# Score products of low queries: over the high keys alone, as pairs of 64-row tiles of the array

## The chip, the cores and the metric

The kernel runs on one core of a Trainium2 chip. The metric is the device time of one execution in microseconds, here the median of several runs.

## What is computed

The reference is an attention over pooled queries, followed by two MLPs in a row. Cut to what matters:

```python
def _attn_ref(q, k, v):                 # q, k, v: (2, 8, 1152, 64)
    q_pool = q.reshape(B, H, S // 2, 2, D).mean(axis=3)
    scores = np.matmul(q_pool, k.transpose(0, 1, 3, 2)) / np.sqrt(D)
    scores = scores - np.max(scores, axis=-1, keepdims=True)
    attn = np.exp(scores)
    attn = attn / (np.sum(attn, axis=-1, keepdims=True) + 1e-09)
    return np.matmul(attn, v)           # (2, 8, 576, 64)
...
x = attn_out.transpose(0, 2, 1, 3).reshape(1152, 512)
x = _moe_ref(x, w_in, w_out)            # ELU between two products, 512 -> 2048 -> 512
return _moe2_ref(x, moe2_w_in, moe2_w_out)   # the same with h * tanh(log(1 + e^h))
```

## The kernel before

The kernel wants more than one rounding to float32r gives. So each operand of a product is split into a high part, the value rounded to float32r, and a low part, what is left of it, and products of the parts are added up in PSUM.

The attention takes the 16 heads in eight pairs (`n`), and each pair in 9 steps (`s` = 9n + t) of 128 queries: steps t = 0 to 3 are queries of the first head, 5 to 8 of the second, and step 4 has 64 of either, for which a block of zeros in the other half is multiplied too. A step has these parts, each a function of class `Attention`:

- `scores` (L298 to L315): the products of the step's 128 queries with all 1152 keys of the head. The keys fall into three chunks, each with its own bank of PSUM: 448 and 450 columns into the two banks of the tile `wide` (two such tiles take turns), and the last 256 into half a bank, `rest` (the halves take turns by steps). The second chunk repeats two keys of the next one.
- `maxima` (L322, L325, on VectorE, DVE): the maximum over `rest` is put beside the other scores, then the maximum over all.
- `exps` (L337 over `rest`, L339 over `wide`, on ScalarE, ACT).
- `turn` and `split_a`: nine transposes per step on TensorE (PE), L370, from the tile `a` to `pst`; their results are split into `th` and `tl` by ACT with DVE or GpSimd (POOL).
- `values` (L410): products with v, 72 per pair, scattered over the steps.

For the scores the head dimension of 64 fills half of the array's 128 rows. The other half is used for the parts of the keys. `KS[h]` holds, for head h, the high parts of the keys in 64 partitions and the low parts in the other 64 (for h = 0 the high ones are partitions 0 to 63, for h = 1 they are 64 to 127); `QH` and `QL` hold the high and the low part of the queries, each stacked twice. So a product of `QH` with `KS` over 128 rows is high queries by high and low keys in one, and that of `QL` with `KS` is low queries by both. A chunk is two products:

```python
            for o, (w, x) in enumerate(ops):
                nc.tensor.matmul(dst, w, x[:, cols], start=(o == 0), stop=(o == len(ops) - 1))
```

`ops` holds `QH` and then `QL` (in step 4 these two for either head), so that a step is six products (twelve in step 4) in the order high, low for each chunk.

`KS` is filled by `stack_k` (L278) with DMAs on SyncE's queue (SP) from tiles `kh` and `kl`, a head at a time, during the pair before: as soon as the last step that reads the old keys is behind. The first pair's keys are written straight by ACT and DVE.

What stands where on each engine is set by a table, `PP['x']`: every piece of work has a due time in steps, and `run` sorts all pieces by it and emits them in that order. The engines PE, ACT, DVE, POOL and SP then run them in order, and wait for one another by semaphores. In the table `W` is the due time of the first two chunks of a step's scores (-1.236 steps) and `R` that of the third (-1.201); nothing of another kind falls between the two in the steps shown. Beside the attention run loads of MLP weights and their conversion from float64 bits (`Weights`), some of them stored to DRAM for later.

The MLPs that follow are bound together by lines L714 (products up) and L734 (down).

Of the kernel before, what the change touches and what calls it, by code (L numbers as in the profile page):

```python
# [10 lines left out]
F32 = mybir.dt.float32  # L11
F32R = mybir.dt.float32r
# [5 lines left out]
PSUM = bass.MemoryType.PSUM  # L18
# [49 lines left out]
    'ncs': 17,  # L68
    'nw': 2,
    'na_': 2,  # L70
    # where each piece of work stands in the order of emission: in steps of 128 queries, for a step, a pair of heads or a weight tile
# [38 lines left out]


class Attention:
    """Two heads at a time; queries j*64+p stand for pooled row 9p+j, keys j*128+p for token 9p+j."""

    def __init__(self, nc, tc, ctx, q, k, v, ident, xh, xl, ps2, ps1):
        self.nc, self.q, self.k, self.v = nc, q, k, v
        self.ident, self.xh, self.xl = ident, xh, xl
        self.ps2, self.ps1 = ps2, ps1
        pool = lambda name, bufs: ctx.enter_context(tc.tile_pool(name=name, bufs=bufs))
        self.raw = pool("raw", 1)  # L120
        self.tmp = pool("tmp", 2)
        self.ap = pool("aprob", PP["na_"])
        self.tiny = pool("tiny", 4)
        self.aTp = pool("aT", 2)
        self.dram = ctx.enter_context(tc.tile_pool(name="dram", bufs=2, space=bass.MemoryType.DRAM))
        fix = pool("fix", 1)
        self.QH = [fix.tile([P, 2, 704], F32R, name=f"qh{i}") for i in range(2)]
        self.QL = [fix.tile([P, 2, 704], F32R, name=f"ql{i}") for i in range(2)]
        self.KS = [fix.tile([P, S], F32R, name=f"ks{h}") for h in range(2)]
        self.VS = [fix.tile([P, 2, NKT, 2, D], F32R, name=f"vs{i}") for i in range(2)]  # L130
        for i in range(2):
            for t in (self.QH[i], self.QL[i]):
                nc.gpsimd.memset(t[:, 0, SQ:].bitcast(F32), 0.0)
        self.pairs = [(b, c) for b in range(B) for c in range(NPAIR)]
        self.rawqk = {}
        self.turned = {}
        self.rawv = {}
        self.qp = {}
        self.kT = {}
        self.wide = {}  # L140
        self.rest = ps1.tile([P, 512], F32, tag="rest", name="rest", bufs=1)
        self.neg = {}
        self.sums = {}
        self.prob = {}
        self.aT = {}
        self.xf = {}
        self.av = {}
        self.avlo = {}
        self.R = {}
        self.rec = {}  # L150
        self.nav = {}
# [12 lines left out]
        self.rawqk[n] = (qr, kr)  # L164

    def warm(self, n):
        """Products that nobody reads, so that TensorE's clock is up when the first heads arrive."""
        nc = self.nc
        z = self.tmp.tile([P, 3, P], F32, name="whole", bufs=PP["nw"])
        nc.vector.memset(z[:], 0.0)  # L170
        zb = z.rearrange("p a b -> p (a b)").bitcast(BF16)
        ps = self.ps2.tile([P, 2, 512], F32, tag="wide", name="wide")
        for i in range(n):
            nc.tensor.matmul(ps[:, 0], zb[:, :P], zb[:, :512], start=True, stop=True)
# [11 lines left out]
        self.nc.vector.tensor_tensor(self.qp[n][heads], qr[:, :, 0, :], qr[:, :, 1, :], op=ALU.add)  # L186

    def split(self, hi, lo, x):
        """hi = x rounded to float32r, lo = what is left, on GpSimd."""
        nc = self.nc  # L190
        nc.gpsimd.tensor_scalar(hi, x, 1.0, 1.0, op0=ALU.mult, op1=ALU.mult)  # L191
        nc.gpsimd.tensor_tensor(lo, x, hi.bitcast(F32), op=ALU.subtract)  # L192
# [42 lines left out]
            nc.vector.tensor_tensor(kl, ps[:, :CH], kh.bitcast(F32), op=ALU.subtract)  # L235

    def first_q(self, h, c, part):
        """The queries of the first pair, a head at a time."""
        nc = self.nc
        key = 0, "q", h, c  # L240
        if part == 0:
            self.turned[key] = ps = self.ps1.tile([P, 512], F32, tag="ps1", name="psq")
            w = 64 + 64 * h
            for i in range(3):
                nc.tensor.transpose(ps[0:64, i * w:(i + 1) * w], self.qp[0][:w, 3 * c + i, :], self.ident[:w, :w])
            return
        src = self.turned[key][0:64, :192 + 192 * h].rearrange("p (j h x) -> p h j x", j=3, x=64)[:, h]
        scale = 0.5 / math.sqrt(D)
        for r in (0,) if h else (0, 64):
            hi, lo = (x[0][r:r + 64, h, 192 * c:192 * c + 192].rearrange("p (j x) -> p j x", x=64) for x in (self.QH, self.QL))  # L250
            if part == 1:
                nc.scalar.activation(hi, src, AF.Copy, scale=scale)
            else:
                nc.vector.scalar_tensor_tensor(out=lo, in0=src, scalar=scale, in1=hi.bitcast(F32),
                                               op0=ALU.mult, op1=ALU.subtract)

    def first_k(self, h, c, part):
        """The keys of the first pair, straight from PSUM."""
        nc = self.nc
        key = 0, "k", h, c  # L260
        m, r = slice(64 * h, 64 * h + 64), slice(64 - 64 * h, 128 - 64 * h)
# [9 lines left out]
            nc.vector.tensor_tensor(self.KS[h][r, cols], self.turned[key][m, :CH], self.KS[h][m, cols].bitcast(F32), op=ALU.subtract)  # L271

    def stack_k(self, n, h):
        """The high and low parts of a head's keys, one above the other."""
        kh, kl = self.kT[n]
        m, r = slice(64 * h, 64 * h + 64), slice(64 - 64 * h, 128 - 64 * h)
        for rows, src in ((m, kh), (r, kl)):
            self.nc.sync.dma_start(self.KS[h][rows, :].bitcast(F32), src[m, :].bitcast(F32))  # L278

    def split_v(self, n, c, part):  # L280
        nc = self.nc
# [10 lines left out]
                (nc.gpsimd if 'vlo' in PP['pl'] else nc.vector).tensor_tensor(lo, vr[:, h, js, :], hi.bitcast(F32), op=ALU.subtract)  # L292

    def part(self, s):
        """Where the scores of the last keys go."""
        return self.rest[:, RW * (s % 2):RW * (s % 2) + RW]

    def scores(self, s, chunks):  # L298
        nc = self.nc
        n, t = divmod(s, 9)  # L300
        QH, QL, KS = self.QH[n % 2], self.QL[n % 2], self.KS
        if t < 4:
            ops = [(Q[:, 0, t * P:(t + 1) * P], KS[0]) for Q in (QH, QL)]
        elif t == 4:
            ops = [(Q[:, 0, 512:640], KS[0]) for Q in (QH, QL)]
            ops += [(Q.rearrange("p h x -> p (h x)")[:, 640:768], KS[1]) for Q in (QH, QL)]
        else:
            ops = [(Q[:, 1, 64 + (t - 5) * P:64 + (t - 4) * P], KS[1]) for Q in (QH, QL)]
        if 0 in chunks:
            self.wide[s] = self.ps2.tile([P, 2, 512], F32, tag="wide", name="wide")  # L310
        for i in chunks:
            cols = (slice(0, WW), slice(WW, 2 * WW + 2), slice(2 * WW, S))[i]
            dst = self.wide[s][:, i, :cols.stop - cols.start] if i < 2 else self.part(s)
            for o, (w, x) in enumerate(ops):
                nc.tensor.matmul(dst, w, x[:, cols], start=(o == 0), stop=(o == len(ops) - 1))  # L315

    def maxima(self, s, part):
        """The maximum of the last keys joins the others' scores, where the second bank repeats a key."""
        nc = self.nc
        wide, rest = self.wide[s], self.part(s)  # L320
        if part == 0:
# [18 lines left out]
                                 bias=neg[:], accum_out=self.sums[n][:, t, 0:1])  # L340

    def reciprocals(self, n, part):
        """1 / (sum + 1e-9), a row of them per head, over the partitions that the head's x has."""
        nc = self.nc
        if part == 0:
            sums = self.sums[n]
# [50 lines left out]
                nc.vector.tensor_tensor(l, src[:, :, x0:x0 + w], h.bitcast(F32), op=ALU.subtract)  # L397

    def values(self, n, g, j0, j1):
        """Some of the keys of one of the four products with v."""  # L400
        nc = self.nc
        h, c0, w = GROUPS[g]
        hi, lo = self.aT[n, g]
# [35 lines left out]
    def run(self, aside):  # L439
# [6 lines left out]
        ev = []  # L446
        add = lambda k, b, f, *a: ev.append((b + X[k], f, a))
        for s in range(T):
            add('W', s, self.scores, s, (0, 1))
            add('R', s, self.scores, s, (2,))  # L450
            add('m', s, self.maxima, s, 0)
            add('M', s, self.maxima, s, 1)
            add('e', s, self.exps, s, 0)
# [47 lines left out]


class Lag:
    """Chains of instructions that follow the products, a link of each chain per step."""

    def __init__(self):
        self.chains = []
# [8 lines left out]


class Weights:
    """Tiles of the float64 weights (MLP m, 0 = in or 1 = out, 128 of the hidden units): to float32, that to two float32r parts."""

    def __init__(self, nc, src, raw, wt, dram, lag):
        self.nc, self.src, self.rawp, self.wt, self.dram, self.lag = nc, src, raw, wt, dram, lag
# [16 lines left out]
        self.loaded[key] = t  # L539

    def chain(self, key, store=False):
        """float64 bits to float32 (clamped to its range), and that to DRAM or to its parts."""
        nc = self.nc
        if key not in self.loaded:
            self.load(key)
# [50 lines left out]
def build(ctx, tc, q, k, v, w1_in, w1_out, w2_in, w2_out, out):  # L596
# [70 lines left out]
        return [link(a, b) for a, b in zip(e, e[1:])]  # L667

    def elu(i, h, gh, gl):
        """max(e^min(h, 0) - 1, h), as e^h - 1 >= h."""  # L670
        e = tmp.tile([P, ZM], F32, name="e")[:, :h.shape[1]]
        return cut([
            lambda: nc.scalar.activation(e[:], h, AF.Relu, scale=-1.0),
# [3 lines left out]
            lambda: nc.vector.tensor_tensor(gl, h, gh.bitcast(F32), op=ALU.subtract)], PP['ec'])  # L677

    def mish(i, h, gh, gl):
        """h * n / (n + 2) with n = e^h (e^h + 2), which is h * tanh(log(1 + e^h))."""  # L680
        e, n, p = (tmp.tile([P, ZM if x == "e" else max(PP['z2'])], F32, name=x)[:, :h.shape[1]] for x in "enp")
        stt = nc.vector.scalar_tensor_tensor
        return cut([
# [138 lines left out]
```

## Time and profile before

| | us |
|---|---|
| median of 3 runs | 702.21 |
| lowest and highest | 702.15, 703.5 |
| span of the profiled execution | 701.6 |
| PE busy in the span | 676.2 |
| DVE busy | 610.0 |
| ACT busy | 484.2 |
| POOL busy | 262.2 |

The profile is of one execution. Its span goes from the first to the last instruction. The attention stage lies between about 12 and 290 us of it, the MLPs behind that. Matmuls overlap one another: a product's recorded time is longer than the distance to the next one's start, and a busy PE may still have room, so that distances between starts are to be read where a cost is wanted. PEld is the load of a product's stationary operand, which runs ahead of the product.

### The profile page before, as it was taken

The numbers are of one execution on the slowest core, as the hardware profiler recorded it, in microseconds if no ns is written. First come the engines' busy times: TensorE is split into PE (matmuls) and PEld (weight loads), VectorE is DVE, ScalarE is ACT, GpSimd is POOL, SyncE is SP. The second block draws the span as 40 slices with busy tenths as digits, with TensorE's granted clock in tenths as the row PEclk, the third lists the DMA queues.
The fourth block names the chain that finished last, engine by engine and source line by source line (L and its number), as shares of the span: only waits on it lengthen the run. The fifth ranks groups of instructions, "written<-read, shape, count | busy, mean of one in ns | idle before, by whom it ended". The sixth has DMA issues, their size and how long they took to land.

```text
span 701.6 us, 12014 instructions
## 1 busy us (share of the span) xinstructions
PE 676.2 (96%) x4043; PEld 613.3 (87%) x4043; DVE 610.0 (87%) x1142; ACT 484.2 (69%) x1180; POOL 262.2 (37%) x328
## 2 busy tenths in 40 slices
PE   7999999999999998799999999999989999999996
PEld 4898989888988897688888999999978999999995
DVE  5899999999999997789798977886999988888884
ACT  5999999999999998575555444666555554445443
POOL 2678787777778787153210000134030000000000
PEclk8999999999999999999999999999999999999999
DMA  8747485867486440456546667565220010002001
GB/s 178 201 119 194 123 199 140 193 172 186 113 198 176 114 141 31 141 191 188 189 149 193 186 185 221 176 195 166 60 75 16 1 45 1 1 0 46 1 1 45
DMA packets 62508, 86.89 MB, mean 124 GB/s; under 512 B 22696, under 2 KB 39152, under 8 KB 62448
## 3 DMA queue, kind: packets, MB, share of 16 engines
q1 hardware_dynamic: 62448, 86.14, 45.3%
q8 instruction: 32, 0.52, 0.3%
q14 instruction: 28, 0.23, 0.1%
HBM read 60.56 MB, written 12.88 MB: 105 GB/s over the span
## 4 chain that ended last, share of the span: by engine, by line
PE 68%; ACT 15%; DVE 10%; issue 3%; DMA 2%; POOL 1%; SPq 0%; ACTq 0%; POOLq 0%
PE acc L734 26%; PE up L714 25%; PE pst L370 5%; PE psv L410 5%; ACT a L339 4%; PE wide L315 3%; ACT whole L385 2%; ACT th L395 2%; ACT a L337 1%; DVE neg L325 1%; ACT wt L555 1%; PE rest L315 1%; DVE tl L397 1%; DVE wt L560 1%; DVE wt L558 1%
## 5 line engine op out<-in xcount | busy, mean ns | idle before, releaser
L714 PE MATMUL up<-xh,wh 128*128 128x384 f32 (+2 forms) x384 | 130.0, 338 | 3.7 <-ACT wh L575 2.7
L714 PE MATMUL up<-xh,wl 128*128 128x384 f32 (+2 forms) x384 | 129.6, 338 | 0.0
L714 PE MATMUL up<-xl,wh 128*128 128x384 f32 (+2 forms) x384 | 129.4, 337 | 0.0
L577 POOL TENSOR_TENSOR wl<-wt,wh 128x512 fp32r<-128x512 f32 x38 | 50.9, 1352 | 208.6 <-ACT wh L575 97.1
L192 POOL TENSOR_TENSOR tl<-whole,th 128x384 fp32r<-128x384 f32 (+1 forms) x112 | 112.2, 1001 | 9.3
L370 PE MATMUL pst<-ident,a 128*128 128x128 f32 x648 | 101.6, 276 | 7.8 <-DVE tl L397 2.6
L370 PEld LDWEIGHTS pst<-ident,a 128*128 128x128 f32 x648 | 75.1, 140 | 19.1 <-ACT a L339 7.7
L410 PE MATMUL psv<-th,vs 128*128 128x256 f32 (+1 forms) x288 | 85.9, 319 | 0.7 <-DVE xf L425 0.5
L714 PEld LDWEIGHTS up<-xh,wh 128*128 128x128 f32 x384 | 72.8, 189 | 8.9 <-ACT wh L575 3.1
L191 POOL TENSOR_SCALAR th<-whole 128x384 fp32r<-128x384 f32 (+1 forms) x112 | 60.6, 541 | 50.7 <-ACT whole L385 50.6
L410 PE MATMUL psv<-tl,vs 128*128 128x256 f32 (+1 forms) x288 | 79.1, 296 | 0.0
L325 DVE TENSOR_REDUCE neg<-wide 128x1 f32<-128x898 f32 x72 | 77.8, 1080 | 0.2
L714 PEld LDWEIGHTS up<-xl,wh 128*128 128x128 f32 x384 | 72.8, 189 | 4.6
L714 PEld LDWEIGHTS up<-xh,wl 128*128 128x128 f32 x384 | 72.6, 189 | 2.9 <-DVE wl L577 0.2
L339 ACT ACTIVATE a<-wide,neg 128x896 f32<-128x896 f32 x72 | 73.3, 1018 | 2.4 <-DVE neg L325 2.0
L687 ACT ACTIVATE e<-n 128x384 f32<-128x384 f32 x48 | 25.2, 526 | 64.9 <-DVE n L686 64.9
L555 ACT ACTIVATE wt<-raw 128x512 f32<-128x512 f32 x64 | 43.3, 679 | 37.8 <-DMA raw<-in_moe_w_out_dram 25.9
L397 DVE TENSOR_TENSOR tl<-pst,th 128x384 fp32r<-128x384 f32 (+1 forms) x128 | 59.9, 497 | 7.6 <-ACT th L395 5.6
L315 PE MATMUL wide<-ks,qh 128*128 128x448 f32 (+1 forms) x160 | 64.9, 406 | 0.0
L734 PE MATMUL acc<-gl,wh 128*128 128x512 f32 (+2 forms) x192 | 64.5, 336 | 0.0
L734 PE MATMUL acc<-gh,wl 128*128 128x512 f32 (+2 forms) x192 | 64.5, 336 | 0.0
L734 PE MATMUL acc<-gh,wh 128*128 128x512 f32 (+2 forms) x192 | 64.4, 335 | 0.0
(89 smaller groups left out, 1695.6 us busy)
## 6 DMA issues: line engine op xcount, KB each, us to landing
raw<-in_moe_w_in_dram SPq DMA_DIRECT2D x32, 512.0 KB, 4.4
raw<-in_moe_w_out_dram SPq DMA_DIRECT2D x32, 512.0 KB, 4.3
w<-wt SPq DMA_DIRECT2D x40, 256.0 KB, 4.1
wt<-w SPq DMA_DIRECT2D x40, 256.0 KB, 2.8
qr<-in_q_dram SPq DMA_DIRECT2D x16, 288.0 KB, 3.9
kr<-in_k_dram SPq DMA_DIRECT2D x16, 288.0 KB, 5.0
vr<-in_v_dram SPq DMA_DIRECT2D x8, 576.0 KB, 3.9
ks<-kh SPq DMA_DIRECT2D x14, 288.0 KB, 3.3
```

What stands on the lines that cost most here:

```text
L191: nc.gpsimd.tensor_scalar(hi, x, 1.0, 1.0, op0=ALU.mult, op1=ALU.mult)
L192: nc.gpsimd.tensor_tensor(lo, x, hi.bitcast(F32), op=ALU.subtract)
L315: nc.tensor.matmul(dst, w, x[:, cols], start=(o == 0), stop=(o == len(ops) - 1))
L325: nc.vector.tensor_reduce(neg[:], wide[:, :, :WW + 1], axis=AX.XY, op=ALU.max, negate=True)
L339: nc.scalar.activation(a[:, :2 * WW].rearrange("p (c x) -> p c x", c=2), wide[:, :, :WW], AF.Exp, bias=neg[:], accum_out=self.sums[n][:, t ...
L370: nc.tensor.transpose(ps[:, i * P:(i + 1) * P], a[:, j * P:(j + 1) * P], self.ident[:])
L397: nc.vector.tensor_tensor(l, src[:, :, x0:x0 + w], h.bitcast(F32), op=ALU.subtract)
L410: nc.tensor.matmul(ps[:, :w], self.VS[n % 2][:, h, j].rearrange("p a d -> p (a d)"), t[:, j, :w], start=(c == 1), stop=(c == 2 * NKT))
L555: lambda: nc.scalar.activation(t[:], high.bitcast(F32), AF.Abs),
L577: e.tensor_tensor(l[:], t[:], h[:].bitcast(F32), op=ALU.subtract)
L714: nc.tensor.matmul(ps[:, :z], w, x, start=(o == 0), stop=(o == len(ops) - 1))
L734: nc.tensor.matmul(ps[:, :x.shape[1]], a, x, start=(i == 0 and o == 0), stop=(i == NFF - 1 and o == 2))
```

## The change

The low queries multiply the high keys only; the product of low queries and low keys is left out, except in the first pair and in step 4 of each pair, where the old products stay. A product of high keys and low queries needs 64 of the array's rows. The first and the third chunk take the rows on which the head's high keys stand in `KS`; for the second chunk a copy of the high keys (450 columns) stands in a new tile `KX` on the other 64 partitions, and `stack_k` fills it with one more DMA for each head of a pair. The products that are 64 rows high carry a tile size of 64 by 128 and a tile position of row 0 or row 64. In all steps the three chunks' products with `QH` now come first and those with `QL` behind them, all at the due time `W`; the entry `R` is gone. The diff without lines that only lose a comment:

```diff
     'x': {
-        'W': -1.236328125, 'R': -1.2011709213256836, 'm': -0.5839824676513672, 'M': 0.07031536102294922, 'e': 0.7480506896972656,
+        'W': -1.236328125, 'm': -0.5839824676513672, 'M': 0.07031536102294922, 'e': 0.7480506896972656,
...
+        self.KX = fix.tile([P, WW + 2], F32R, name="kx")
...
         for rows, src in ((m, kh), (r, kl)):
             self.nc.sync.dma_start(self.KS[h][rows, :].bitcast(F32), src[m, :].bitcast(F32))
+        self.nc.sync.dma_start(self.KX[r, :].bitcast(F32), kh[m, WW:2 * WW + 2].bitcast(F32))
...
-    def scores(self, s, chunks):
+    def scores(self, s):
...
         if t < 4:
-            ops = [(Q[:, 0, t * P:(t + 1) * P], KS[0]) for Q in (QH, QL)]
+            ops = [(0, lambda Q: Q[:, 0, t * P:(t + 1) * P])]
         elif t == 4:
-            ops = [(Q[:, 0, 512:640], KS[0]) for Q in (QH, QL)]
-            ops += [(Q.rearrange("p h x -> p (h x)")[:, 640:768], KS[1]) for Q in (QH, QL)]
-        else:
-            ops = [(Q[:, 1, 64 + (t - 5) * P:64 + (t - 4) * P], KS[1]) for Q in (QH, QL)]
-        if 0 in chunks:
-            self.wide[s] = self.ps2.tile([P, 2, 512], F32, tag="wide", name="wide")
-        for i in chunks:
-            cols = (slice(0, WW), slice(WW, 2 * WW + 2), slice(2 * WW, S))[i]
-            dst = self.wide[s][:, i, :cols.stop - cols.start] if i < 2 else self.part(s)
-            for o, (w, x) in enumerate(ops):
-                nc.tensor.matmul(dst, w, x[:, cols], start=(o == 0), stop=(o == len(ops) - 1))
+            ops = [(0, lambda Q: Q[:, 0, 512:640]), (1, lambda Q: Q.rearrange("p h x -> p (h x)")[:, 640:768])]
+        else:
+            ops = [(1, lambda Q: Q[:, 1, 64 + (t - 5) * P:64 + (t - 4) * P])]
+        self.wide[s] = self.ps2.tile([P, 2, 512], F32, tag="wide", name="wide")
+        cols = (slice(0, WW), slice(WW, 2 * WW + 2), slice(2 * WW, S))
+        dst = [self.wide[s][:, 0, :WW], self.wide[s][:, 1, :WW + 2], self.part(s)]
+        todo = []
+        for h, q in ops:
+            for i in range(3):
+                todo.append((i, q(QH), KS[h][:, cols[i]]))
+        for h, q in ops:
+            m, r = slice(64 * h, 64 * h + 64), slice(64 - 64 * h, 128 - 64 * h)
+            for i in range(3):
+                if n == 0 or t == 4:
+                    todo.append((i, q(QL), KS[h][:, cols[i]]))
+                elif i == 1:
+                    todo.append((i, q(QL)[r], self.KX[r, :]))
+                else:
+                    todo.append((i, q(QL)[m], KS[h][m, cols[i]]))
+        left = [sum(x[0] == i for x in todo) for i in range(3)]
+        full = list(left)
+        for i, w, x in todo:
+            nc.tensor.matmul(dst[i], w, x, start=(left[i] == full[i]), stop=(left[i] == 1))
+            left[i] -= 1
...
-            add('W', s, self.scores, s, (0, 1))
-            add('R', s, self.scores, s, (2,))
+            add('W', s, self.scores, s)
```

On PE, in a step of the second head of the third pair (the products of the step follow the last transposes of a pair's queries, L199), before (`ks_114` is `KS[1]`, `qh_109` and `ql_111` are `QH` and `QL` of the even pairs):

```order
L370 MATMUL pst<-ident,a 128x128 x6
L199 MATMUL psq<-ident,qp 64x128 x6
L370 MATMUL pst<-ident,a 128x128 x3
L315 MATMUL wide<-ks_114,qh_109 128x448
L315 MATMUL wide<-ks_114,ql_111 128x448
L315 MATMUL wide<-ks_114,qh_109 128x450
L315 MATMUL wide<-ks_114,ql_111 128x450
L315 MATMUL rest<-ks_114,qh_109 128x256
L315 MATMUL rest<-ks_114,ql_111 128x256
```

And the same place of the changed kernel:

```order
L386 MATMUL pst<-ident,a 128x128 x6
L200 MATMUL psq<-ident,qp 64x128 x6
L386 MATMUL pst<-ident,a 128x128 x3
L330 MATMUL wide<-ks_114,qh_109 128x448
L330 MATMUL wide<-ks_114,qh_109 128x450
L330 MATMUL rest<-ks_114,qh_109 128x256
L330 MATMUL wide<-ks_114,ql_111 128x448
L330 MATMUL wide<-kx,ql_111 128x450
L330 MATMUL rest<-ks_114,ql_111 128x256
```

The three high products moved ahead of the three low ones, and the low product of 450 columns reads `kx`; what stands around the six is the same.

On SP's queue, where the keys of the second pair are stacked for its second head, before (`raw` and `w` belong to the MLP weights, `vr` is v, `qh` and `ql` are the queries' second copy):

```order
L535 DMA raw_611<-in_moe_w_in_dram 128x4x256
L216 DMA qh1_110<-qh1_110 64x2x576
L216 DMA ql1_112<-ql1_112 64x2x576
L582 DMA w0_0_4_641<-wt_459 128x512
L278 DMA ks1_114<-kh_305 64x1152
L278 DMA ks1_114<-kl_306 64x1152
L179 DMA vr_763<-in_v_dram 128x2x576
```

And in the changed kernel:

```order
L280 DMA kx_115<-kh_306 64x450
L550 DMA raw_613<-in_moe_w_in_dram 128x4x256
L217 DMA qh1_110<-qh1_110 64x2x576
L217 DMA ql1_112<-ql1_112 64x2x576
L597 DMA w0_0_4_643<-wt_460 128x512
L279 DMA ks1_114<-kh_306 64x1152
L279 DMA ks1_114<-kl_307 64x1152
L280 DMA kx_115<-kh_306 64x450
L180 DMA vr_766<-in_v_dram 128x2x576
```

One copy to `kx` stands behind the two copies to `ks` of each head, and ahead of a load of weights or of v; the rest of the queue has its old order. PE's first reader of `kx` in each head, steps 0 and 5, waits for that copy. DVE, ACT and POOL have the same instructions in the same order as before.

## Rows read from the trace of the kernel before

**Rows 1.** The page: span, and the chain that ended last by engine.

```profile
span 701.6 us, 12014 instructions
...
PE 68%; ACT 15%; DVE 10%; issue 3%; DMA 2%; POOL 1%; SPq 0%; ACTq 0%; POOLq 0%
```

**Rows 2.** Stages: us from:to, length, busy us of each engine, clock, DMA share, GB/s.

```profile
300.00:700.00 400.00, 393.54 (x2124) 359.24 (x2122) 336.45 (x637) 215.73 (x455) 50.92 (x38) 1.00 0.34 101
```

**Rows 3.** One period in stretches; busy us: PE, PEld, DVE, ACT, POOL.

```profile
79.50:83.10 3.60, 3.60 (x28) 3.53 (x27) 3.09 (x9) 3.34 (x10) 3.23 (x5) 1.00 0.27 41
83.10:86.50 3.40, 3.40 (x28) 3.32 (x27) 3.34 (x7) 3.20 (x9) 1.89 (x3) 1.00 0.39 152
86.50:90.00 3.50, 3.50 (x30) 3.44 (x29) 3.50 (x6) 3.31 (x10) 3.33 (x5) 1.00 0.61 171
...
98.50:102.30 3.80, 3.44 (x24) 2.54 (x22) 3.52 (x9) 3.76 (x14) 1.93 (x4) 1.00 0.99 222
102.30:105.80 3.50, 3.50 (x25) 3.42 (x26) 3.31 (x9) 3.23 (x11) 2.64 (x6) 1.00 0.43 99
105.80:109.00 3.20, 3.20 (x25) 3.13 (x24) 3.20 (x6) 2.97 (x9) 1.81 (x3) 1.00 0.43 93
```

**Rows 4.** The chain in order of time: start us, us, engine, tile, line, count.

```profile
46.97 0.81 PE wide L315 x4
...
80.07 0.81 PE wide L315 x4
...
87.59 1.00 ACT a L339 x2
...
102.80 0.82 PE wide L315 x4
...
274.75 0.82 PE wide L315 x4
```

**Rows 5.** Timeline of PE: start us, us, then what, [idle before].

```profile
102.25 0.55 PE L370 MATMUL pst<-ident,a 128*128 128x128 f32 x3
...
103.04 0.37 PE L315 MATMUL wide<-ks,qh 128*128 128x450 f32 x1
103.25 0.37 PE L315 MATMUL wide<-ks,ql 128*128 128x450 f32 x1
103.45 0.28 PE L315 MATMUL rest<-ks,qh 128*128 128x256 f32 x1
103.57 0.28 PE L315 MATMUL rest<-ks,ql 128*128 128x256 f32 x1
103.69 0.32 PE L410 MATMUL psv<-th,vs 128*128 128x320 f32 x1
...
104.57 0.49 PE L370 MATMUL pst<-ident,a 128*128 128x128 f32 x3
...
106.96 0.28 PE L315 MATMUL rest<-ks,qh 128*128 128x256 f32 x1
...
109.28 0.45 PE L315 MATMUL wide<-ks,qh 128*128 128x448 f32 x1
```

**Rows 6.** Timeline of PEld, the loads, where the columns of the array change.

```profile
116.42 0.09 PEld L353 LDWEIGHTS psr<-ident,rec 128*9 128x9 f32 x1
116.52 0.19 PEld L315 LDWEIGHTS wide<-ks,qh 128*128 128x128 f32 x1
...
127.14 0.25 PEld L199 LDWEIGHTS psq<-ident,qp 128*64 128x64 f32 x3 [0.56 <-ACT whole L385]
127.39 0.36 PEld L370 LDWEIGHTS pst<-ident,a 128*128 128x128 f32 x3
```

**Rows 7.** Timeline of ACT, the exponentials over `rest`.

```profile
105.55 0.48 ACT L337 ACTIVATE a<-rest,neg 128x256 f32<-128x256 f32 x1
```

**Rows 8.** SP's timeline at a copy of the keys, and L278's time to landing.

```profile
96.54 0.54 SPq L278 DMA_DIRECT2D ks<-kl  x1
...
DMA to landing us min/median/max: 3.1/5.0/7.9
```

## The prediction, made before the changed kernel ran

> **What bounds the kernel now.** I read the page's first lines and its chain first [rows 1]. TensorE (PE) holds 68% of the chain that ended last, ScalarE (ACT) 15%, VectorE (DVE) 10%. The change touches only the score products of the attention stage, 12 to 275 us of the span; the MLPs behind it, where PE is busy 393.54 of 400 us [rows 2], see none of it and only move with the stage's end. So the question is what bounds the attention stage. That stage repeats itself every 33.1 us, a pair of heads in 9 steps. I took one such period in stretches of a step or two and compared the busy time of the engines in each [rows 3]: in 79.5 to 86.5 us and in 102.3 to 109 us PE is busy all the time, in 86.5 to 90 us PE (3.50 of 3.50) and DVE (3.50) both are, in 98.5 to 102.3 us PE idles 0.36 us while ACT is busy 3.76 of 3.80. The chain of waits says the same [rows 4]: in the period it runs through the score products at 80.07 and 102.80 us (and again one step after each), and through ACT's exponentials at 87.59 us in between. The bound alternates: PE for about 15 of 33 us, ACT for most of the rest, with DVE hardly behind.
>
> The reader is to see two things there. PE's time is worth something, but only in the steps whose score products lie on the chain. From 46.97 us, the first in a pair that the change touches, to 274.75 us the chain has 23 pieces "PE wide L315 x4"; the first and the last stand in [rows 4]. The changed products are in 56 steps (7 pairs with 8 steps each; the first pair and the fifth step of each pair keep the old form).
>
> **What is removed: 450 columns per step, if the pair runs side by side.** The six products of a step start 0.20 us apart with 448 or 450 columns (103.04, 103.25, 103.45) and 0.12 us apart with 256 (103.45, 103.57, 103.69) [rows 5]. The three low ones so cost 0.20 + 0.20 + 0.12 = 0.52 us. After the change the 448- and the 256-column products use one half of the array's rows, the 450-column one the other half. If the halves work at the same time, the first half needs 0.20 + 0.12 = 0.32 us. The second half needs its own weights: loads of 128 columns can follow each other 0.10 to 0.11 us apart (116.42 to 116.52 [rows 6]), so it ends at 0.11 + 0.20 = 0.31 us, inside the first half's time. That saves 0.20 us of PE per step. No trace here shows two products side by side, so this is the bound on the good side; on the other there is no saving, since in-order products of 64 rows have as many columns as before. I take the good side for the likeliest, because the two write different banks and read different partitions, so nothing in the program orders them.
>
> **What is added: two changes of the array's shape per step.** From 128 rows to 64 ahead of the low products, and back behind them. The nearest rows are changes of the number of columns: the load of the transposes at 127.39 us follows the three 64-column loads at 127.14 us, and the 128-column load at 116.52 us follows that of 9 columns at 116.42 us [rows 6]. The three loads of 64 columns take 0.25 us to the next shape's load, 0.10 us from the 9-column one to the next: the pace of loads within one shape, and no idle time is printed on either row. By these a change of shape costs nothing, and I take 0. Changes of the number of rows happen before only in the first pair's start, always behind a wait, and tell nothing. The other bound is that PE must run empty at each change. A 256-column product is recorded for 0.28 us while the next one starts after 0.12 us [rows 5]: a tail of 0.16 us that would be laid open. Then the first load is uncovered as after a wait: three transposes take 0.55 us behind one (102.25) and 0.49 us without (104.57) [rows 5], 0.06 us. That is 0.22 us per change, 0.44 us per step.
>
> The Trainium skill (TensorEngine Tiling, Array Packing; Key Properties) says that changing the tiling mode, not just the tile, drains the TensorE. The column changes above don't agree with it as a general rule; for rows no trace here shows it. By the rule the sum would be that of rival 1.
>
> **What is moved.** The low products come behind all high ones, so the last-keys product with the high queries is third instead of fifth, 0.4 us earlier. It waits for ACT to have read the same half of that bank two steps before. In one step ACT's activation starts at 105.55 us and takes 0.48 us, and the product starts at 106.96 us [rows 5, 7]: 0.93 us spare, 0.5 left. No cost. The last product of the step stays the same, so DVE's maxima, which need all three banks, start no earlier within the step. DVE's, ACT's and GpSimd's own instructions keep their order.
>
> **KX.** Each pair brings two more DMAs of 115 KB on SP's queue, behind the copies of the keys (L278). One such issue takes 0.54 us of the queue and a copy of 288 KB lands in 3.1 to 7.9 us [rows 8]. The first head's last copy is issued at 96.54 us, so KX would be at about 97.1 us and there by 105.0 us even at 7.9; its first reader is in the step that starts at 109.28 us [rows 5]. 14 copies of 0.115 MB are 1.6 MB of 86.9, so I put the traffic at nothing. The second head's reader is five steps away. If that cover were gone, its price is SP's 0.54 us twice per pair, 7.6 us in all at the very most.
>
> **The sum.** 23 steps on the chain by 0.20 us are 4.6 us, the most that this chain can give. What is late next is DVE or ACT. In 79.5 to 86.5 us two steps save 0.40 us, ACT has 0.46 us of idle time there and DVE 0.57 [rows 3]: all of it can be had. In 102.3 to 109 us they save 0.40 us, ACT has 0.50 us, but DVE only 0.19: half. So 0.59 of 0.80 us is left, 4.6 x 0.59 / 0.80 = 3.4 us. An engine that leads still idles a little (ACT is busy 3.31 of 3.50 us in 86.5 to 90 us, where the chain is on it [rows 3, 4]), so not all of this room can be filled; I take three quarters, a choice: 2.6 us. The span before is 701.6 us [rows 1] and the median 702.2, 0.6 us apart; taking the saving off the median gives 699.6 us. The case spans 697.6 us (all 4.6) to 701.5 us.
>
> **Rivals.**
> 1. Row changes drain the array: +0.44 - 0.20 = +0.24 us of PE per step. The 23 steps on the chain pay 5.5 us. Of the other 33, two in a pair (14) are covered by PE's idle time, as in 98.5 to 102.3 us; 19 have none (86.5 to 90 us: 3.50 of 3.50) and pay 0 to 4.6 us. So 5.5 to 10 us, about 7: 709 us. It decides from 0.10 us per change on, where two changes eat the 0.20 us. [...] Against it: the column changes cost nothing.
> 2. The pair doesn't run side by side, and the changes are cheap: the change doesn't do what it says, PE does the same 1154 columns, only in another order: 702.2 us. The same comes out if a change costs about 0.1 us or if DVE takes over everywhere: within 1.4 us.
> 3. KX or the earlier last-keys product becomes a wait: up to 7.6 us by the bound above, more likely 2: 704 us. The margins of 4 us and 0.5 us speak against it.
>
> The Trainium skill (TensorE: Matmul & The Clock Gate, Part 3) reports that products in different row groups start about 4 ns apart and that four of 32 rows ran 3.07 times as fast. No run here shows it; by it the pair would again take 0.32 us with the third product.
>
> **How the numbers follow.** The forecast has 0.45, drains 0.30, no saving 0.20, KX or the moved product 0.05. The kernel's runs can tell about 0.2%, 1.4 us. Faster by more: 0.40 of the forecast's 0.45, and 0.03 of the others. Within it: 0.05 of the forecast, 0.17 of the others. Slower: 0.29 of the drains, 0.06 of the others. So 0.43, 0.22, 0.35. The range runs from 697.6 us to 708.5 us, which leaves out the upper half of the drains, about 0.15, and little below; the forecast's own is 697.6 to 701.5 us.
>
> **What would show it.** Right: the 450-column low product starts at most 0.11 us behind the 448-column one, the three low ones and the next product's start lie 0.3 us apart, the load behind them comes without idle time, and fewer pieces of the chain are score products. Rival 1: 0.2 us of empty PE between the third high and the first low product, and again before the next transposes. Rival 2: low products 0.20 us apart. Rival 3: waits of PE on a DMA or on ACT at the scores. If the attention stage shortens and the MLPs begin no earlier, the sum was made in the wrong place.

## The result: slower by 0.7%

| | us |
|---|---|
| before, median of 5 runs | 702.54 (702.15 to 703.5) |
| after, median of 5 runs | 707.59 (705.67 to 710.55) |
| ratio, with its 95% interval | 1.0067 [1.0044, 1.0089] |
| span of the profiled execution after, and its own time | 703.8, 705.67 |

The forecast was 699.6 us, faster. The measured time lies inside the whole range (697.6 to 708.5 us) and outside the forecast's own (697.6 to 701.5 us); it is near the 709 us of rival 1, the drained array. The profiled execution is the fastest of the five.

The page of the kernel after, to be held against [rows 1]: the span, and the chain that ended last by engine.

```profile
span 703.8 us, 12022 instructions
...
PE 71%; ACT 14%; DVE 8%; DMA 4%; issue 2%; SPq 0%; POOL 0%; ACTq 0%
```

PE's share of the chain has grown, from 68% to 71%, where the forecast wanted fewer score products on it. The place to look at is a step. This is the timeline of PE after (start us, us, what), the same step as in [rows 5]:

```profile
102.48 0.55 PE L386 MATMUL pst<-ident,a 128*128 128x128 f32 x3
102.79 0.65 PE L330 MATMUL wide<-ks,qh 128*128 128x448 f32 x2
103.27 0.28 PE L330 MATMUL rest<-ks,qh 128*128 128x256 f32 x1
103.48 0.47 PE L330 MATMUL wide<-ks,ql 64*128 64x448 f32 x1
103.48 0.47 PE L330 MATMUL wide<-kx,ql 64*128 64x450 f32 x1
103.79 0.28 PE L330 MATMUL rest<-ks,ql 64*128 64x256 f32 x1
104.00 0.41 PE L426 MATMUL psv<-th,vs 128*128 128x320 f32 x1
104.25 0.31 PE L426 MATMUL psv<-tl,vs 128*128 128x320 f32 x1
104.39 0.31 PE L426 MATMUL psv<-th,vs 128*128 128x320 f32 x1
```

And the loads of the same stretch, PEld:

```profile
103.08 0.19 PEld L330 LDWEIGHTS rest<-ks,qh 128*128 128x128 f32 x1
103.48 0.18 PEld L330 LDWEIGHTS wide<-ks,ql 64*128 64x128 f32 x1 [0.21 <-issue]
103.48 0.18 PEld L330 LDWEIGHTS wide<-kx,ql 64*128 64x128 f32 x1
103.59 0.19 PEld L330 LDWEIGHTS rest<-ks,ql 64*128 64x128 f32 x1
103.99 0.19 PEld L426 LDWEIGHTS psv<-th,vs 128*128 128x128 f32 x1 [0.22 <-POOL tl L193]
104.10 0.19 PEld L426 LDWEIGHTS psv<-tl,vs 128*128 128x128 f32 x1
```

The loads of the same place before; the two products ahead of them start at 103.45 and 103.57 us [rows 5]:

```profile
103.45 0.19 PEld L315 LDWEIGHTS rest<-ks,ql 128*128 128x128 f32 x1
103.57 0.19 PEld L410 LDWEIGHTS psv<-th,vs 128*128 128x128 f32 x1
```

Two things stand there side by side. The pair works as hoped: both products start at 103.48 us, even their loads do, and the third low product starts 0.31 us after the first, where three in line take 0.51 us from the first start to the third (the run without the pair, below). That saves 0.20 us. But the loads stop at both changes of the number of rows. The loads of the pair begin 0.21 us after the last high product has started, and the load of the values product begins 0.20 us after the last low product's start (103.79 to 103.99); before, each of the two loads begins at the very start of the product ahead, and its own product follows 0.12 us later. Each time the first load is then uncovered. With free changes the second values product would start 0.12 + 0.20 + 0.12 + 0.15 us behind 103.27, at 103.86 us; it starts at 104.25. The two changes cost 0.39 us, the pair saves 0.20. PE's own rows show no gap there: the last high product is recorded until 103.55 us (103.27 + 0.28), so the stop is to be seen in the loads and in the starts, and that the array stood empty isn't shown.

The waits of the loads between 20 and 290 us (who waited for what: us in total, times, longest) show how regular that is. These rows have no counterpart of that size before:

```profile
PEld wide L330 <- issue: 12.2, 55, 0.2
...
PEld psv L426 <- issue: 4.2, 19, 0.3
...
PEld psv L426 <- ACT whole L401: 2.6, 12, 0.2
PEld psk L224 <- issue: 2.2, 10, 0.2
...
PEld psv L426 <- POOL tl L193: 0.9, 4, 0.2
```

("issue" stands where the engine waited for nothing that the profile shows.) The first is the change to 64 rows, 55 times 0.22 us in 56 steps. The others are changes back, 45 in these rows. They are 0.22 us each on average whoever is named behind them, nobody 29 times, ACT 12 times and GpSimd 4 times, as in the step above; a stop of the same length under three names has one cause, and the named one only came before it.

### The profile page after: what moved, and what is told of

The parts are those of the page before. It is cut to its first block, busy times and chain, and to the rows that moved or that the text cites. A ratio compares the mean times of both kernels' runs of the same rounds, so it can differ in the third digit from the quotient of the medians.

```text
span 703.8 us, 12022 instructions
## 1 busy us (share of the span) xinstructions
PE 680.9 (97%) x4043; PEld 597.3 (85%) x4043; DVE 609.4 (87%) x1142; ACT 486.3 (69%) x1180; POOL 262.4 (37%) x328
## 4 chain that ended last, share of the span: by engine, by line
PE 71%; ACT 14%; DVE 8%; DMA 4%; issue 2%; SPq 0%; POOL 0%; ACTq 0%
PE acc L749 24%; PE up L729 23%; PE psv L426 9%; PE pst L386 7%; PE wide L330 5%; ACT a L355 3%; ACT th L411 2%; DMA raw<-in_moe_w_out_dram 2%; ACT whole L401 2%; PE rest L330 2%; PE psq L200 1%; DVE wt L573 1%; DMA kx<-kh 1%; ACT wh L590 1%; DVE wt L575 1%
## 5 line engine op out<-in xcount | busy, mean ns | idle before, releaser
L426 PE MATMUL psv<-th,vs 128*128 128x256 f32 (+1 forms) x288 | 88.7, 329 | 0.5 <-DVE xf L441 0.5
L426 PEld LDWEIGHTS psv<-th,vs 128*128 128x128 f32 x288 | 54.3, 188 | 8.8 <-issue 4.2
```

Of the source, the lines that this page charges most:

```text
L426: nc.tensor.matmul(ps[:, :w], self.VS[n % 2][:, h, j].rearrange("p a d -> p (a d)"), t[:, j, :w], start=(c == 1), stop=(c == 2 * NKT))
```

## The experiments

Each kernel was timed against the kernel before on its own chip; ratios refer to that. The runs of the kernel before spread from 699.9 to 706.1 us over all chips, so that differences under about 1 us are not read.

**Order and copies alone.** The order-only kernel takes the old products everywhere and has no KX; the second one keeps the copies to KX, unread:

```diff
-                if n == 0 or t == 4:
+                if True:
```

> The changed order (three high products, then three low ones, all at W) with every product over 128 rows; no KX and no copy to it. If the row changes cause the loss, nothing of it is left: 702.5 us, within 0.2% of the kernel before. If the order does (the last-keys product two places earlier, the banks finished closer together), the loss stays: about 707 us. If the copies to KX do: 702.5 us too.

> As the order-only kernel, with the 14 copies to KX, which nobody reads. If the copies are innocent: 702.5 us, as the order-only kernel. If SP's queue or the traffic causes the loss: 704 to 707 us, with KX or what stands behind it on the chain of waits.

Measured: 703.85 us against 702.5, ratio 1.0010 [0.9994, 1.0025], and 703.14 us, 1.0008 [0.9995, 1.0021]. Neither the order nor the copies are worth anything that can be told from noise. The period of a pair, from the first score product of the third pair to that of the fourth, is 33.12 us in both traces, against 33.10 us before. So the loss comes with the products of 64 rows, or with waits of their readers for KX, which nobody reads here. The trace of the kernel after has no wait of PE for `kx`. One of the copies stands on its chain (issued at 213.94 us, landed 6.87 us later), but what follows it there, ACT's copy of `row`, starts at 220.71 us, before that landing and without a gap behind ACT's work ahead of it: nothing waited. And the next kernel has no KX and loses more.

**64 rows, but one after the other.**

```diff
                 elif i == 1:
-                    todo.append((i, q(QL)[r], self.KX[r, :]))
+                    todo.append((i, q(QL)[m], KS[h][m, cols[i]]))
```

> The low products over 64 rows, but all three on the rows of the head's high keys in KS, so one after the other; no KX. The two row changes of a step stay, the working side by side goes. Row changes as the cause: PE pays 0.20 us more per step than the changed kernel, 0.37 us more than the kernel before, in 56 steps 20 us of PE's time; of this some 60% showed in the end before (4.7 us of 9.5 us), so about 702.5 + 12 = 714 us. If the row changes are cheap and the pair itself is slow (two streams in each other's way): 702 to 704 us.

Measured: 714.47 us, ratio 1.0172 [1.0150, 1.0194], as the row changes had it. The timeline of PE shows the same two stops around three products in line:

```profile
105.19 0.28 PE L328 MATMUL rest<-ks,qh 128*128 128x256 f32 x1
105.40 0.67 PE L328 MATMUL wide<-ks,ql 64*128 64x448 f32 x2
105.91 0.27 PE L328 MATMUL rest<-ks,ql 64*128 64x256 f32 x1
106.11 0.42 PE L424 MATMUL psv<-th,vs 128*128 128x320 f32 x1
```

0.21 and 0.20 us, as in the changed kernel, and 0.51 us from the first low product to the third instead of 0.31. So working side by side is a real gain of 0.20 us a step, and the two changes take back more than it. That the total came out as expected is partly luck: 4.7 of 9.5 us, the figures behind the expected share of 60%, are half. Measured are 12 of 56 x 0.39 = 22 us.

**Four changes instead of two.**

```diff
+        if len(todo) == 6 and n > 0:
+            todo = [todo[0], todo[1], todo[3], todo[4], todo[2], todo[5]]
```

> The changed kernel with the third chunk's high product moved between the low pair and the last low product, so that a step has four row changes instead of two; columns and pairs as in the changed kernel. If each change empties the array, at 0.18 to 0.19 us each, PE pays 0.37 us more per step, 0.54 us more than the kernel before, 30 us in 56 steps; at the share of the unpaired kernel (12 us of 21 us) that is 17 to 20 us: about 720 us. If only the first change of a step, or the waiting for the second set of weights, costs: 708 to 712 us.

Measured: 726.14 us, ratio 1.0341 [1.0313, 1.0369], more than expected. The loads, PEld:

```profile
105.55 0.18 PEld L332 LDWEIGHTS wide<-ks,ql 64*128 64x128 f32 x1 [0.31 <-issue]
105.55 0.18 PEld L332 LDWEIGHTS wide<-kx,ql 64*128 64x128 f32 x1
105.95 0.19 PEld L332 LDWEIGHTS rest<-ks,qh 128*128 128x128 f32 x1 [0.22 <-ACT th L413]
106.27 0.18 PEld L332 LDWEIGHTS rest<-ks,ql 64*128 64x128 f32 x1
106.58 0.31 PEld L388 LDWEIGHTS pst<-ident,a 128*128 128x128 f32 x3
```

Every change has its stop, in both directions: a single 256-column product between two changes holds the array from 105.95 to 106.27 us and from 106.27 to 106.58, 0.31 to 0.32 us instead of 0.12. That is 0.19 to 0.20 us per change, measured without any other step of the argument.

**Where the chain ran, and where not.** Pairs only in half of the steps, old products in the rest:

```diff
-                if n == 0 or t == 4:
+                if n == 0 or t not in (1, 2, 7, 8):    # the other kernel: (0, 3, 5, 6)
```

> Paired low products only in the steps whose score products lie on the chain of waits before (t = 1, 2, 7, 8: 28 of the 56), the others over 128 rows. If PE's time counts where the chain runs through it: nearly all of the loss, 28 x 0.17 = 4.8 us, so 706 to 707 us. If it counts everywhere alike: half, 705 us.

> The complement: paired low products only in t = 0, 3, 5, 6. If PE's time counts only on the chain: 702.5 to 703.5 us. If everywhere alike: half of the loss, 705 us.

Measured: 705.49 us, ratio 1.0036 [1.0015, 1.0057], and 704.94 us, 1.0040 [1.0024, 1.0056]. By the total it counts everywhere alike. The period of a pair in the traces, taken as above, says otherwise: it is 33.10 us before, 33.81 in the first of the two kernels, 33.27 in the second and 33.94 after. There 0.71 of the 0.84 us come from the steps on the chain. But the periods of the fifth and seventh pair, which are longer before (34.97 us, with a load of v and one of weights on the chain of waits), are 33.83 and 33.69 us in the first kernel: there it gains 2.42 us, much of what it loses in the other pairs. From the first score product of the second pair to the MLPs' first product it is 243.85 us before, 244.78 in the first kernel, 243.93 in the second and 247.02 after. So in the trace of the second kernel the attention stage is hardly longer than before; the stretch of the MLPs is (416.3 us for 414.7). That the fifth and seventh pair wait for loads is seen in the trace of before; why they stop doing so with a slower PE, and why the totals are alike, wasn't tried and stays open. In the kernel after these two periods are 34.63 and 34.62 us, 0.34 us shorter than before, so that the 0.84 us hold for the other periods only.

**What saved PE time is worth, without any row change.** The first kernel leaves one low product out, the second all three:

```diff
+                if n > 0 and t != 4 and i == 1:    # the other kernel: without "and i == 1"
+                    continue
```

> Leaves out the low product of the second chunk in the 56 steps (its scores lack the low queries), the others over 128 rows, no KX: 0.20 us of PE's time less per step and no row change, what the change would have given with free changes. By the sum on record 2.6 us less than before, 699.9 us, 4.6 us at the most; if DVE and ACT are as near as the busy times say, 1 us or less.

> Leaves out all three low products in the 56 steps (their scores lack the low queries): 0.52 us of PE's time less per step, no row change. Without the low product of the second chunk the attention stage was 3.4 us shorter, but the MLPs 2.4 us longer. If DVE and ACT bound the attention there, it ends only a little earlier than with that, 4 to 5 us before the kernel before; if PE still does, 8 us. If the MLPs wait for their weights whatever happens ahead of them, the whole stays at 700 to 702.5 us; if not, it falls to 697 us or less.

Measured: 701.99 us against 702.5, ratio 0.9997 [0.9981, 1.0013], and 700.62 us against 702.74, 0.9976 [0.9956, 0.9997]. The period of a pair is 32.52 us in the one and 32.55 us in the other: 0.32 us less of PE in each of eight steps brings nothing more. The stretches of one period, in the view of [rows 3], for the first and the second of these kernels:

```profile
75.70:108.20 32.50, 31.55 (x227) 28.33 (x225) 31.46 (x60) 31.81 (x89) 26.16 (x36) 1.00 0.70 168
```

```profile
74.10:106.70 32.60, 30.08 (x212) 25.88 (x210) 31.49 (x60) 31.81 (x89) 26.11 (x36) 1.00 0.71 168
```

PE's busy time falls from 31.55 to 30.08 us, ACT stays at 31.81 and DVE at 31.5 us of it: they are the floor. Put together, with PE's time per step against the kernel before (-0.52 and -0.20 us for the products left out, 0.39 - 0.20 = +0.19, +0.39 without the pair, 2 x 0.39 - 0.20 = +0.58 with four changes), in eight steps of a pair:

| kernel | PE's time per pair, us | period of the pair, us | against before |
|---|---|---|---|
| no low products | -4.2 | 32.55 | -0.55 |
| no second low product | -1.6 | 32.52 | -0.58 |
| before | 0 | 33.10 | 0 |
| changed | +1.5 | 33.94 | +0.84 |
| one after the other | +3.1 | 35.22 | +2.12 |
| four changes | +4.6 | 36.78 | +3.68 |

PE's time is worth less the more of it is taken away, and more the more is added: the kernel before stands in the bend between a stage bound by ACT and DVE and one bound by PE.

**Where the saved time went.** With one low product left out, the MLPs' first product starts at 283.18 us instead of 286.93, but the stretch from there to the end is 417.1 us instead of 414.7. In the trace PE has a wait in the first MLP that it doesn't have before, and the repeat of this kernel (below) has it too, with 1.3 us:

```profile
PE acc L749 <- DVE gl L692: 1.5, 1, 1.5
```

(`gl` is the low part of what the first MLP's ELU gives.) DVE is late there because it stands behind ACT's conversion of weight tiles, and ACT behind their loads. This is the conversion ahead of the wait in the timeline of ACT, with the product left out:

```profile
435.12 0.66 ACT L570 ACTIVATE wt<-raw 128x512 f32<-128x512 f32 x1 [3.03 <-DMA raw<-in_moe_w_in_dram]
```

And the same one before:

```profile
437.30 0.66 ACT L555 ACTIVATE wt<-raw 128x512 f32<-128x512 f32 x1 [2.88 <-DMA raw<-in_moe_w_in_dram]
```

It comes 2.18 us earlier, while the MLPs start 3.75 us earlier: the loads don't keep up. To test that, two of these tiles were moved out of the first MLP, in this kernel and in the kernel before, by two entries of the table `c2`, which names the weight tiles that are converted early and stored to DRAM for later:

```diff
-    'c2': {..., '27': 29, '29': 29, '31': 31, '30': 17, ...},
+    'c2': {..., '27': 29, '30': 17, ...},
```

> Leaves out the low product of the second chunk in the 56 steps, as the earlier kernel did whose attention stage was 3.4 us shorter by its periods and whose whole was 0.5 us shorter; and two of the second MLP's weight tiles (entries 29 and 31 of the table of early stores) are no longer converted during the first MLP, but where the second needs them. If the chain of weight loads and conversions in the first MLP takes back the rest, this kernel is 3 us or more below the next one (the kernel before with the same two tiles moved). If the rest goes elsewhere, 0.5 to 1 us below it.

> The kernel before with the same two weight tiles moved, as the base for the other. The wait that the other showed at the third part of the first MLP isn't on the chain here, so 702 to 703 us.

> The kernel without the low product of the second chunk once more, on the same chip as the two others. 0.5 us below the kernel before, as the first time, if it is no accident; 3 us if it was.

Measured on one chip: 700.87 us (ratio 0.9975 [0.9954, 0.9996]) with the product left out and the tiles moved, 704.03 us (1.0023 [1.0004, 1.0042]) for the kernel before with the tiles moved, and 701.82 us (0.9994 [0.9975, 1.0014]) for the repeated kernel. So 3.2 us of difference with the tiles moved and 0.5 us without, twice, which can't be told from nothing. That is what the expectation asks of the weights' chain, but it doesn't show that the chain takes back the rest. Moving the tiles costs 1.7 us by itself in the kernel before, and that makes up half of the 3.2 us; with the product left out it is only 0.95 us better than without moving them, within the intervals. And the kernel before with the tiles moved has, in its trace (its slowest execution, 707.42 us), a loss of its own in the first MLP:

```profile
PE acc L734 <- DVE xl L745: 4.0, 2, 3.5
```

(`xl` is the low part of a result of the MLP; the longest of these waits is 3.5 us.) It ends at 387.7 us, and behind it TensorE's granted clock has a mean of 0.66 from 387 to 392 us, that is, in part its lower level of 1.2 GHz. The kernel without any low product speaks against a fixed loss, too: from the second pair on its attention stage is 3.1 us shorter than before (240.7 for 243.85 us; 3.8 us with one product left out), and 2.1 us of that are in the total. So with one product left out most of the attention's saving doesn't arrive, in two runs; that the weights' loads take it is likely by the wait above and isn't shown.

## Why the prediction was wrong

- **The bound.** That PE and ACT take turns, with DVE hardly behind, held for the period: the steps on PE's part of the chain carry 0.71 of 0.84 us. That PE's time is worth something only in those steps isn't borne out by the totals, where pairs in the other steps cost as much (1.0040 against 1.0036).
- **The pair.** The side I chose held: both products start together, and the saving of 0.20 us is the one expected (0.31 us from the first low product to the third for 0.51 us in line). That 0.31 us lies so near the 0.32 us of the prediction is an accident: the 0.32 us ran to the product behind the third one, and the 0.31 us hold an uncovered load of 0.11 us. Without the pair the kernel is 7 us slower still (714.47 against 707.59).
- **The row changes: the step that failed.** I took them at nothing, by the rows in which the number of columns changes [rows 6]. Those were the nearest rows by name only: a column change doesn't stop the loads, a row change does. Measured are 0.39 us per step, 0.19 to 0.20 us per change. The bound from the tail of 0.16 us and the uncovered load of 0.06 us was 0.22 [rows 5], near in the sum and off in its parts: the stop adds 0.09 us (0.21 us behind a 256-column product for 0.12) and the uncovered load 0.10 to 0.11 us. The point from which rival 1 decides was put at 0.10 us, and the change stands at twice that. The sentence of the Trainium skill (TensorEngine Tiling, Array Packing; Key Properties) that changing the mode drains the TensorE agrees with the traces for rows in that a change costs time, 0.19 to 0.20 us; an empty array they don't show. For columns rows 6 show no such stop.
- **The moved product and KX.** Both at nothing, and the runs with these alone are within 0.1%. KX's copies land in 4.0 to 7.0 us; each takes SP 0.77 to 1.21 us, not the 0.54 us put on it, and nothing waited for them.
- **The sum.** The attention stage's side of it was right in size: 2.6 us, 4.6 at the most, were worked out, and 3.8 us came when one product a step was taken away. That the period gave 0.58 us where 0.59 us of room per pair was worked out is partly luck, since the 0.59 us were those of four steps and the 0.58 us came with eight. Three things behind it were not right. It was carried to the end as if nothing stood behind the stage; of the 3.8 us only 0.5 arrived, so by these two runs free row changes would have given about 0.5 us, not 2.6. It was priced with 23 steps of one trace for both signs, while the period moves by 0.36 us per us of PE taken and 0.55 us per us added. And the profiled execution is not 0.6 us but about 1.9 us above its span, as the kernel after's (705.67 and 703.8) shows, so the profile of before (703.5 us by that) is one of its slower runs.
- **The size of the loss.** Rival 1 had 5.5 to 10 us with 0.24 us per step; it was 5 us with 0.19. In the spans only 2.2 us of it show: the stretch from the second pair's first score product to the MLPs is 3.2 us longer, but it began 1.11 us earlier in the profile of after (41.97 for 43.08 us). The first pair has the old products in both kernels, but from 10 to 14 us TensorE was granted its lower level before (0.50, which is 1.2 GHz) and its full one after (1.00, 2.4 GHz). Ahead of that PE ran the first pair's transposes in both, with waits of up to 0.67 us. The rows of before, then of after:

```profile
10.00:14.00 4.00, 3.64 (x15) 3.17 (x16) 2.58 (x6) 3.22 (x10) 2.43 (x5) 0.50 0.61 153
...
10.00:14.00 4.00, 3.29 (x23) 2.84 (x24) 3.45 (x8) 3.63 (x12) 2.52 (x5) 1.00 0.62 161
```

This goes with the execution and not with the change: of the two kernels without pairs, order alone has 1.00 in this stretch and starts its second pair at 41.61 us, order and copies 0.50 and 43.12 us. The rest of the 5 us isn't seen in these two executions. That the runs of after spread over 5 us, more than those of before on that chip, is left open.

## What to carry to other kernels

Row tiles pay by working side by side, and cost at each change of the number of rows: here 0.19 us a change, about the streaming time of one product of 450 columns. So they don't pay in a group of three between full products. With more pairs between a change and the one back it would be different: by these figures two pairs (0.40 us) make up for the two changes (0.39 us), an estimate that no run here tests. And before PE's time is valued, it is to be seen what ends the stage without it, and what waits behind the stage: here the other two engines allowed 0.58 us a pair, and with one product left out most of that didn't reach the total.

## What was unexpected of the hardware

A change from 128 to 64 rows or back held the next load for 0.20 to 0.22 us from the start of a 256-column product, in either direction, while changes from 64 or 9 columns back to 128 showed no stop [rows 6]. With four changes a step, one of them comes behind a product of 450 columns, and its load starts 0.30 us after that product; both times that is 0.09 us more than to the next product's start in one shape (0.12 and 0.20 us [rows 5]). The loads of two row halves start together, as the two products do (103.48 us for all four), although in a running row of loads each follows the one ahead by 0.10 us or more [rows 6].
